# Key-query products of two chunks on four quarters of TensorE, in two PSUM banks, and a new search of the order

## The chip, the cores and the metric

The kernel runs on one core of one Trainium2 chip. Its time is the device time of one execution in microseconds; the lower, the better. A core has TensorE (PE in the profile, with its weight loads as PEld), VectorE (DVE), ScalarE (ACT), GpSimd (POOL) and SyncE (SP), which here only issues DMAs. Each engine works through its own list of instructions in the order in which they were written, and waits on semaphores where an operand is not there yet.

## The reference

Two stages in one kernel: a gated linear attention (4 batches, 8 heads, 768 steps, head size 48), then a gated convolution with a matmul, and a normalised two-layer network with a residual (model width 384, inner width 1536).

```python
f = 1.0 / (1.0 + np.exp(-f_logit))
for t in range(S):
    state = f[:, :, t, :, None] * state + np.einsum('bhd,bhe->bhde', k[:, :, t], v[:, :, t])
    y[:, :, t] = np.einsum('bhd,bhde->bhe', q[:, :, t], state)
...
x = np.ascontiguousarray(attn_out.transpose(0, 2, 1, 3)).reshape(B, S, H * D)
gate = 1.0 / (1.0 + np.exp(-gate_pre))      # gate_pre: causal convolution of x, 5 taps
x = gate * (x @ w_val) @ w_out
xn = (x - mu) / np.sqrt(var + 1e-06) * g_ln
return x + np.maximum(xn @ w_ch1, 0.0) @ w_ch2
```

## The kernel before

The 3072 tokens are cut into 24 attention tiles of 128 tokens and 12 groups of 256 tokens; a group is two tiles. A tile has two chunks of 64 tokens (`c`), four pairs of heads (`n`), and the two heads of a pair (`hh`), one on partitions 0 to 47 and one on 64 to 111.

Attention per tile. `prep` brings gates, keys and queries into the form with features on the partitions (on PE for the first eight tiles, on DVE after that) and makes `ft`, `kt`, `mv`, `gs`, `fc` on DVE, with two scans per tile. `at_t` turns `kt` on PE; ACT copies the result to `kn`. `at_a` makes the key-query products: for each chunk, pair and head one fp32 matmul with 64 columns of `kt` as weights and 64 columns of `mv` moving, 16 in all, all into one PSUM bank; ACT copies each half of the bank (64 partitions by 512) over `mv`, and POOL masks it (`affine_select`). `at_d` makes the increments of the state (16 matmuls of 48 columns) and runs the recurrence over chunks on DVE and POOL. `at_y` multiplies both by the values and the state (16 matmuls, two heads side by side in the columns, over 112 or 128 rows). An fp32 matmul is two MATMUL records in the trace, so each of these blocks is 32 of them.

Network per group. `gates` is the convolution, on DVE (12 operations of 128 x 256). `val` and `x1` are the two matmuls of the gated stage, `xnt` turns the normalised rows and ACT and DVE split them in `nh` and `nl`. `c1` and `c2` are the two layers, each product as three fp32r matmuls of full width (high by high, high by low, low by high): 18 of 256 columns and 12 of 384 for each of six slices of the inner width. Between them ACT makes `hidden_hi` and DVE `hidden_lo` out of the same bank. The weights arrive as 64-bit floats and are converted on ACT, DVE and POOL (`stage`, `wt`, `w_hi`, `w_lo`) while the first groups run.

What sets the order. The program is recorded as units (`Plan`), and a planner with a price for each unit (`price`), a delay for each dependence (`wait`) and eight PSUM banks lists the units of all engines by a greedy simulation (`forward`), eight passes back and forth, then once more with the ranks of some stretches moved by the table `MOVED`. The order so found is what each engine executes; the banks that units get come out of it too. Transposes, products, sums: everything passes through one helper, so all of it has line 466 in the profile, and rows are told apart by their tiles.

In the words below, a *block* is the 32 MATMUL records of one `at_a` (key-query), `at_d` (state) or `at_y` (output); the other matmuls use the full width of PE. A *visit* is a stretch of one or more blocks with full-width matmuls on both sides.

Of the kernel before, what the change touches and what calls it, by code (L numbers as in the profile page):

```python
# [22 lines left out]
NP = H // 2  # L23
# [29 lines left out]
WARM = 1.03  # L53
SWITCH = 0.12
# [53 lines left out]
class Unit:  # L108


    def __init__(self, engine):
        self.costs = dict.fromkeys(engine.split("|"), 0.0)
        self.engine = next(iter(self.costs))
        self.calls = []
        self.delay = self.margin = 0.0
        self.deps = set()
        self.opens = None
        self.uses = set()
        self.port = False
# [13 lines left out]
class Plan:  # L133
# [43 lines left out]
    def record(self, engine, method, args, kw):  # L177
# [25 lines left out]
        for x, writes in [(x, False) for x in ins] + ([(out, True)] if on_chip(out) else []):  # L203
            r = self.region(x)
            if isinstance(r.name, int) and r.name not in u.uses:
                if not self.users[r.name]:
                    u.opens = r.name
                else:
                    u.deps.add(self.users[r.name][0])
                u.uses.add(r.name)  # L210
                self.users[r.name].append(me)
# [15 lines left out]
        if engine == "tensor" and not u.costs["tensor"] and ins[0].dtype != F32R:  # L227
            u.costs["tensor"] = SWITCH
# [16 lines left out]
    def price(self, engine, method, out, ins, n, args, kw):  # L245
        if engine == "tensor":
            if method == "transpose":
                return 0.105 * self.slow
            if ins[0].dtype == F32R:
                return (0.436e-3 * n + 0.006) * self.slow  # L250
            return (0.056 if n > D else 0.043) * self.slow
# [35 lines left out]
    def transfer(self, issued, u, out, in_):  # L287
# [9 lines left out]
        u.costs = {"wire": n / run * (11.0 + (0.0595 if run < 1024 else 0.053 if run < 2048 else 0.0705) * run) / 16e3}  # L297
# [40 lines left out]
    def forward(self, deps, users, rank):  # L338
# [13 lines left out]
        ends = [0.0] * len(held)  # L352

        def start(i, e):
# [4 lines left out]
            if u.opens is not None:  # L359
                first = sorted(banks.values())  # L360
                spare = 1 if e == "vector" else 0
                t = max(t, first[spare]) if len(first) > spare else NEVER
# [19 lines left out]
        while len(order) < len(units):  # L382
            best = None
            for e in ENGINES:
                for i in waiting[e]:
                    t = (start(i, e), ready[i] if e == "wire" else rank[i])
                    if (best is None or t < best[0]) and fits(i, e):
                        best = (t, i, e)
# [8 lines left out]
            end[i] = free[e] = t + u.costs[e]  # L397
# [4 lines left out]
            if u.opens is not None:  # L402
                homes[u.opens] = min(banks, key=banks.get)
                del banks[homes[u.opens]]
# [64 lines left out]
class Kernel:  # L469
# [313 lines left out]
    def at_a(self, a):  # L783
        nc = self.nc
        kt, mv = self.kt[a % 2], self.mv[a % 2]
        pa = self.bank().rearrange("p (c n t) -> p c n t", c=NC, n=NP)
        with self.unit():
            for c in range(NC):
                for n in range(NP):
                    for hh in range(2):  # L790
                        r = slice(64 * (1 - hh), 64 * (1 - hh) + D)
                        nc.tensor.matmul(
                            pa[64 * hh : 64 * hh + 64, c, n, :],
# [5 lines left out]
        for hh in range(2):  # L799
            r = slice(64 * hh, 64 * hh + 64)  # L800
            nc.scalar.copy(mv[r, hh], pa[r])
# [429 lines left out]
```

## Time and profile before

| | |
|---|---|
| time, median of 3 runs | 538.26 us (537.22 to 538.6) |
| time of the profiled execution | 538.87 us |
| its span, first to last instruction | 537.2 us |
| mean granted clock of TensorE | 0.99 |
| PE busy | 501.3 us (93%) |
| PEld busy | 477.9 us (89%) |
| DVE busy | 369.1 us (69%) |
| ACT busy | 270.6 us (50%) |
| POOL busy | 169.5 us (32%) |
| share of PE in the chain that ended last | 71% |

The span has two stretches: one until the first layer of the network starts (about 81 us), in which inputs and weights arrive and several engines wait for each other, and the rest. A matmul's duration in a row is longer than its place in the stream, because matmuls are pipelined: the distance from one start to the next is what each costs.

### The profile page before, as it was taken

The page shows a single profiled execution, that of the slowest core. Times are in us where ns is not written, and L with a number is a line of the kernel's source. Part 1 is how long each engine was busy: PE and PEld are TensorE (multiplying, and loading weights), DVE is VectorE, ACT ScalarE, POOL GpSimd, SP SyncE. Part 2 cuts the span into 40 slices and gives each one's busy share as a digit, 9 for nine tenths or more (in the row PEclk, how much of TensorE's full clock was granted, in tenths as well). Part 3 has the DMA queues.
Part 4 walks back from the last instruction along what each step waited for, and adds up shares of the span by engine and source line. Part 5 has one row for each costly group of instructions (what it writes and reads, how often), then busy time and mean ns, then how long its engine had stood idle before and what let it go on. Part 6 is the DMA issues. An engine that isn't in the chain of part 4 may idle for free.

```text
span 537.2 us, 13413 instructions
## 1 busy us (share of the span) xinstructions
PE 501.3 (93%) x5272; PEld 477.9 (89%) x5272; DVE 369.1 (69%) x737; ACT 270.6 (50%) x591; POOL 169.5 (32%) x312
## 2 busy tenths in 40 slices
PE   2987689999999999999999999999999999999994
PEld 1776579999999999999989999999989999999993
DVE  5898989999884975874889733985793542543411
ACT  2598879995472453453486222543552542512210
POOL 3365676245340422230277001231421431300000
PEclk9998989999999999999999999999999999999998
DMA  6985786973454234133143610162110100000001
GB/s 137 177 172 106 190 214 173 234 227 83 103 145 94 51 85 92 39 100 70 38 114 73 149 47 1 31 156 60 24 39 9 23 31 2 9 31 1 29 1 35
DMA packets 94560, 45.60 MB, mean 85 GB/s; under 512 B 56341, under 2 KB 94485, under 8 KB 94490
## 3 DMA queue, kind: packets, MB, share of 16 engines
q1 hardware_dynamic: 94490, 44.67, 34.8%
q8 instruction: 43, 0.70, 0.6%
q14 instruction: 27, 0.22, 0.2%
HBM read 38.75 MB, written 4.72 MB: 81 GB/s over the span
## 4 chain that ended last, share of the span: by engine, by line
PE 71%; DVE 12%; DMA 4%; POOL 4%; ACT 3%; issue 2%; SPq 2%; DVEq 0%; POOLq 0%; ACTq 0%
PE ps L466 71%; DVE ps L466 4%; SPq L466 2%; POOL rs L466 2%; DVE mv L466 2%; DMA raw_q<-in_q 1%; DVE wt L466 1%; DMA xt<-x 1%; DMA stage<-in_moe_w_ch 1%; DVE gs L466 1%; ACT xn L466 1%; DVE bns L466 1%; DMA raw_f<-in_f_logit 1%; DMA out_x<-x 1%; DVE nl L466 1%
## 5 line engine op out<-in xcount | busy, mean ns | idle before, releaser
L466 PE MATMUL ps<-nh,w_hi 128*128 128x256 f32 x432 | 123.5, 286 | 0.4 <-DVE nl L466 0.3
L466 PE MATMUL ps<-nl,w_hi 128*128 128x256 f32 x432 | 121.1, 280 | 0.4 <-DVE nl L466 0.3
L466 PE MATMUL ps<-nh,w_lo 128*128 128x256 f32 x432 | 120.9, 280 | 0.0
L466 PE MATMUL ps<-w_hi,hidden_hi 128*128 128x384 f32 x288 | 99.3, 345 | 0.0
L466 DVE SCALAR_TENSOR_TENSOR hidden_lo<-ps,hidden_hi 128x512 fp32r<-128x512 f32 x72 | 49.2, 684 | 70.3 <-ACT hidden_hi L466 70.2
L466 PE MATMUL ps<-w_hi,hidden_lo 128*128 128x384 f32 x288 | 96.9, 337 | 0.0
L466 PE MATMUL ps<-w_lo,hidden_hi 128*128 128x384 f32 x288 | 96.8, 336 | 0.0
L466 ACT ACTIVATE hidden_hi<-ps 128x512 fp32r<-128x512 f32 x72 | 42.9, 595 | 85.7 <-PE ps L466 84.4
L466 PEld LDWEIGHTS ps<-nh,w_hi 128*128 128x128 f32 x432 | 81.3, 188 | 1.8 <-DVE nl L466 0.5
L466 PEld LDWEIGHTS ps<-nh,w_lo 128*128 128x128 f32 x432 | 82.1, 190 | 0.0
L466 PEld LDWEIGHTS ps<-nl,w_hi 128*128 128x128 f32 x432 | 81.2, 188 | 0.9 <-DVE nl L466 0.9
L466 DVE SCALAR_TENSOR_TENSOR ps<-xt,convw,ps 128x256 f32<-128x256 f32 x144 | 65.7, 483 | 3.5 <-ACT ps L466 1.8
L466 POOL TENSOR_SCALAR_AFFINE_SELECT mv<-mv 64x512 f32<-64x512 f32 x48 | 32.2, 671 | 86.6 <-ACT mv L466 84.9
L466 PEld LDWEIGHTS ps<-w_hi,hidden_hi 128*128 128x128 f32 x288 | 54.1, 188 | 1.1
L466 PEld LDWEIGHTS ps<-w_lo,hidden_hi 128*128 128x128 f32 x288 | 54.2, 188 | 0.0
L466 PEld LDWEIGHTS ps<-w_hi,hidden_lo 128*128 128x128 f32 x288 | 54.1, 188 | 0.0
L466 POOL TENSOR_TENSOR sd<-sn,fc 112x192 f32<-112x192 f32 x43 | 22.7, 529 | 69.8 <-DVE sn L466 54.9
L466 ACT COPY kn<-ps 64x192 f32<-64x192 f32 x96 | 30.1, 313 | 14.1 <-PE ps L466 12.9
L466 DVE TENSOR_TENSOR_SCAN gs<-ps,ends 128x511 f32<-128x511 f32 x24 | 29.1, 1214 | 9.3 <-ACT ps L466 8.9
L466 DVE TENSOR_TENSOR mv<-ps,ft 64x512 f32<-64x512 f32 x48 | 33.0, 688 | 2.5 <-PE ps L466 1.0
L466 PE MATMUL ps<-xh,wv_hi 128*128 128x256 f32 x108 | 32.7, 302 | 0.9 <-DVE gt L466 0.9
L466 PE MATMUL ps<-xl,wv_hi 128*128 128x256 f32 x108 | 31.4, 291 | 0.0
(102 smaller groups left out, 993.8 us busy)
## 6 DMA issues: line engine op xcount, KB each, us to landing
stage<-in_moe_w_ch SPq DMA_DIRECT2D x24, 384.0 KB, 4.5
st<-in_v SPq DMA_DIRECT2D x96, 48.0 KB, 2.5
out_x<-x SPq DMA_DIRECT2D x24, 192.0 KB, 1.9
raw_f<-in_f_logit SPq DMA_DIRECT2D x32, 96.0 KB, 2.3
raw_k<-in_k SPq DMA_DIRECT2D x32, 96.0 KB, 2.3
raw_q<-in_q SPq DMA_DIRECT2D x32, 96.0 KB, 2.4
raw_f<-in_f_logit SPq DMA_DIRECT2D x32, 80.0 KB, 2.2
raw_k<-in_k SPq DMA_DIRECT2D x32, 80.0 KB, 2.4
```

The source lines that it names most:

```text
L466: getattr(getattr(self.nc, engine), method)(*args, **kw)
```

## The change

Three things.

First, `at_a` opens two banks, one for each chunk, and gives the second chunk the other two of PE's four 64 x 64 quarters: output partitions are `64 * (c ^ hh)` and up, where they were `64 * hh` and up for both chunks. The loop runs over pairs outside and chunks inside, so that four matmuls that follow each other go to four quarters. ACT empties each of the four pieces by a copy of 64 x 256, where it made two copies of 64 x 512.

Second, the planner's model: it charges a change of PE's tiling (`TILING`, at the moment of the change, by mode: full width, quarters, halves) where it charged each such unit 0.12; it prefers units in the mode that PE is in (`STAY`); a unit can open more than one bank; a matmul with at most 48 rows is priced 0.03, not 0.056 or 0.043; transposes 0.102, not 0.105; full-width matmuls a little less (`WARM`); DMA a little slower.

Third, the table `MOVED` was searched anew under that model, which changes the order on every engine.

```diff
-WARM = 1.03
-SWITCH = 0.12
+WARM = 1.01
+TILING = (0.117, 0.092, 0.092)
+STAY = 3.0
...
 MOVED = (
-    (416, 8, -12), (2566, 20, -8), (22, 6, 5), (1533, 20, -20), (1524, 40, 8), (1231, 3, 8),
+    (1, 6, -5), (25, 12, 8), (156, 1, 8), (183, 12, 20), (316, 2, -5), (342, 6, 12), (387, 4, 2),
...
-        if engine == "tensor" and not u.costs["tensor"] and ins[0].dtype != F32R:
-            u.costs["tensor"] = SWITCH
+        if engine == "tensor" and method == "matmul" and ins[0].dtype != F32R:
+            u.mode = 1 if ins[0].ap[0][1] <= 64 else 2
...
-                return 0.105 * self.slow
+                return 0.102 * self.slow
...
-            return (0.056 if n > D else 0.043) * self.slow
+            return (0.03 if len(ins) and ins[0].ap[0][1] <= D else 0.056 if n > D else 0.043) * self.slow
...
+        def cost(i, e):
+            u = units[i]
+            return u.costs[e] + (TILING[u.mode] if e == "tensor" and u.mode != mode else 0.0)
+
+        def urgency(i, e):
+            if e == "wire":
+                return ready[i]
+            return rank[i] + (STAY if e == "tensor" and units[i].mode != mode else 0.0)
...
-        pa = self.bank().rearrange("p (c n t) -> p c n t", c=NC, n=NP)
+        pa = [self.bank()[:, 0 : NP * C].rearrange("p (n t) -> p n t", n=NP) for c in range(NC)]
+        half = lambda c, hh: slice(64 * (c ^ hh), 64 * (c ^ hh) + 64)
         with self.unit():
-            for c in range(NC):
-                for n in range(NP):
+            for n in range(NP):
+                for c in range(NC):
                     for hh in range(2):
                         r = slice(64 * (1 - hh), 64 * (1 - hh) + D)
                         nc.tensor.matmul(
-                            pa[64 * hh : 64 * hh + 64, c, n, :],
+                            pa[c][half(c, hh), n, :],
                             kt[r, n, c * C : c * C + C],
                             mv[r, hh, c, n, :],
                             start=True,
...
-            nc.scalar.copy(mv[r, hh], pa[r])
+            for c in range(NC):
+                nc.scalar.copy(mv[r, hh, c], pa[c][half(c, hh)])
```

How the order moves, at three places. Names: `mv`, `kt`, `st`, `kn` are the operands of the blocks, `xh`, `wv` those of `val`, `xn` the normalised rows, `ps_` a PSUM bank. On PE, around the key-query block of the ninth tile, before:

```order
L466 MATMUL ps_161<-w_5_hi,hidden_lo 128x384
L466 MATMUL ps_158<-ident,xn_145 128x128 x3
L466 MATMUL ps_159<-ident,kt_116 128x112 x4
L466 MATMUL ps_161<-mv_114,kt_116 64x64 x16
L466 MATMUL ps_158<-xh,wv_hi 128x256
L466 MATMUL ps_158<-xl,wv_hi 128x256
```

and on PE around the block of the same tile now (the two rows of banks 160 and 157 repeat four times):

```order
L483 MATMUL ps_157<-ident,xn_145 128x128 x3
L483 MATMUL ps_158<-mv_115,st_113 48x64 x16
L483 MATMUL ps_161<-ident,xn_146 128x128 x3
L483 MATMUL ps_160<-mv_114,kt_116 64x64 x2
L483 MATMUL ps_157<-mv_114,kt_116 64x64 x2
...
L483 MATMUL ps_158<-st_112,kn_121 48x48 x16
L483 MATMUL ps_163<-ident,kt_117 128x112 x4
L483 MATMUL ps_161<-nh_147,w_0_hi 128x256
```

The key-query block stood alone between full-width matmuls; now it alternates between two banks, and the state block of the same tile follows it directly, in one visit. Counted from the first `c1` matmul on, 52 blocks made 50 visits before and make 36 now: of the 16 joins now, 11 are between key-query or state blocks, or between two output blocks, and 5 between an output block and one of the others; before there was one of each. In both orders 7 key-query blocks stand ahead of the first `c1` matmul and 17 behind it.

On DVE, ahead of the second `nl` (the last operand that the first `c1` matmul waits for), before:

```order
L466 SCALAR_TENSOR_TENSOR gs<-ps_160,ends 128x511
L466 TENSOR_TENSOR nl_149<-ps_163,nh_147 128x3x128
L466 TENSOR_TENSOR kt_117<-ps_161,gs 128x512
L466 TENSOR_TENSOR gt<-gt,ps_157 128x256
L466 TENSOR_TENSOR nl_149<-ps_164,nh_147 128x3x128
```

and on DVE at the same place now:

```order
L483 SCALAR_TENSOR_TENSOR gs<-ps_163,ends 128x511
L483 TENSOR_TENSOR gt<-gt,ps_161 128x512
L483 TENSOR_TENSOR nl_149<-ps_160,nh_147 128x3x128
L483 SCALAR_TENSOR_TENSOR wt<-ps_162,wt 128x384
L483 TENSOR_TENSOR kt_117<-ps_158,gs 128x512
L483 TENSOR_SCALAR lows<-gs 128x8
L483 CAST w_0_hi<-wt 128x2x192
L483 RECIPROCAL starts<-lows 128x8
L483 TENSOR_TENSOR gt<-gt,ps_161 128x256
L483 SCALAR_TENSOR_TENSOR wt<-ps_162,wt 128x384
L483 SCALAR_TENSOR_TENSOR ft<-ps_163,starts 128x512
L483 TENSOR_TENSOR nl_149<-ps_162,nh_147 128x3x128
```

The scan to `ft` and the parts before it have moved ahead of the second `nl`. Not counting the memsets at the start, 128 instructions stood ahead of that `nl` on DVE and 133 do now: in come a scan to `ft` with its `lows` and `starts`, a subtraction to `xl`, one of 128 x 512 to `gl`, one to `wv_lo`, a combination to `wt` and two shifts to `wt`; out go a rounding to `w_hi`, two subtractions to `w_lo` and an addition to `sn`. Ahead of the eighth `hidden_lo` it was 215 and is 227; on ACT, ahead of the eighth `hidden_hi`, 211 and 232, with one more load of its function table.

On ACT, at the first key-query block, before:

```order
L466 ACTIVATE ps_162<-ps_162 128x512
L466 COPY st_112<-sd_126 48x192
L466 COPY mv_114<-ps_158 64x512 x2
L466 COPY kn_122<-ps_157 64x192 x3
L466 ACTIVATE ps_159<-ps_159 128x512
```

and on ACT at the same place now:

```order
L483 ACTIVATE ps_163<-ps_163 128x512
L483 COPY mv_114<-ps_159 64x256
L483 COPY mv_114<-ps_158 64x256
L483 COPY st_112<-sd_126 48x192
L483 COPY mv_114<-ps_159 64x256
L483 COPY kn_122<-ps_161 64x192 x4
L483 COPY mv_114<-ps_158 64x256
```

Two copies have become four, and other copies stand between them.

## Rows read from the trace of the kernel before

**Rows 1.** Busy time of each engine in three stretches: bounds, length, then engines.

```profile
0.00:81.00 81.00, 56.96 (x849) 48.85 (x849) 68.57 (x141) 57.44 (x132) 43.80 (x89) 0.96 0.77 165
81.00:125.00 44.00, 43.40 (x363) 42.61 (x358) 42.83 (x93) 42.06 (x91) 20.11 (x27) 1.00 0.74 201
125.00:529.20 404.20, 400.62 (x4067) 386.38 (x4065) 256.47 (x502) 171.12 (x371) 105.57 (x197) 1.00 0.23 57
```

**Rows 2.** Timeline around the start of the first layer: start, duration, engine, what.

```profile
80.30 0.56 DVE L466 TENSOR_TENSOR nl<-ps,nh 128x384 fp32r<-128x384 f32 x1 [0.36 <-ACT nh L466]
...
81.05 0.38 PE L466 MATMUL ps<-nh,w_hi 128*128 128x256 f32 x1
```

**Rows 3.** Timeline of PE around a key-query block that stands alone.

```profile
247.37 0.34 PE L466 MATMUL ps<-w_lo,hidden_hi 128*128 128x384 f32 x1
247.54 0.34 PE L466 MATMUL ps<-w_hi,hidden_lo 128*128 128x384 f32 x1
247.81 1.15 PE L466 MATMUL ps<-mv,kt 48*64 48x64 f32 x32
...
249.17 0.34 PE L466 MATMUL ps<-w_lo,hidden_hi 128*128 128x384 f32 x1
```

**Rows 4.** Timeline of PE from 247.75 to 247.85: what has started by then.

```profile
247.81 0.27 PE L466 MATMUL ps<-mv,kt 48*64 48x64 f32 x2
```

**Rows 5.** Timeline of PE: four transposes of 112 columns.

```profile
251.08 0.55 PE L466 MATMUL ps<-ident,kt 112*128 112x112 f32 x4
```

**Rows 6.** Timeline of PE from 24.1 to 25.0: an early block, waiting for its second head.

```profile
24.22 0.32 PE L466 MATMUL ps<-mv,kt 48*64 48x64 f32 x2
```

**Rows 7.** Timeline of PE: an output block, whose two heads share their rows.

```profile
241.31 1.10 PE L466 MATMUL ps<-mv,st 112*48 112x64 f32 x32
```

**Rows 8.** Timeline of PE around a state block that stands alone.

```profile
253.44 0.28 PE L466 MATMUL ps<-nh,w_lo 128*128 128x256 f32 x1
253.65 0.92 PE L466 MATMUL ps<-st,kn 64*48 64x48 f32 x32
...
254.72 0.29 PE L466 MATMUL ps<-nl,w_hi 128*128 128x256 f32 x1
```

**Rows 9.** Timeline of PE around a state and a key-query block in one visit.

```profile
393.81 0.28 PE L466 MATMUL ps<-nh,w_lo 128*128 128x256 f32 x1
394.02 0.92 PE L466 MATMUL ps<-st,kn 64*48 64x48 f32 x32
394.77 1.11 PE L466 MATMUL ps<-mv,kt 48*64 48x64 f32 x32
...
396.04 0.29 PE L466 MATMUL ps<-nl,w_hi 128*128 128x256 f32 x1
```

**Rows 10.** Groups by line and shape, DVE: busy, mean ns | idle before.

```profile
L466 DVE TENSOR_TENSOR_SCAN ft<-ps,starts 128x512 f32<-128x512 f32 x24 | 29.1, 1214 | 0.4
...
L466 DVE TENSOR_TENSOR sn<-sd,ps 112x192 f32<-112x192 f32 x44 | 15.2, 345 | 15.0 <-POOL sd L466 7.3 <-PE ps L466 6.4 <-ACT gh L466 1.1
...
L466 DVE TENSOR_SCALAR wt<-stage 128x384 uint16<-128x384 uint16 x13 | 6.4, 492 | 0.1
...
L466 DVE RECIPROCAL starts<-lows 128x8 f32<-128x8 f32 x24 | 4.5, 186 | 0.2
L466 DVE TENSOR_TENSOR w_lo<-wt,w_hi 128x384 fp32r<-128x384 f32 x8 | 4.4, 546 | 0.0
...
L466 DVE TENSOR_TENSOR gl<-gt,gh 128x512 fp32r<-128x512 f32 x6 | 4.1, 688 | 2.1 <-ACT gh L466 2.1
...
L466 DVE TENSOR_TENSOR xl<-xt,xh 128x768 fp32r<-128x768 f32 x2 | 1.9, 944 | 0.1
```

**Rows 11.** Groups by line and shape, ACT: two copies out of PSUM, and the table.

```profile
L466 ACT COPY kn<-ps 64x192 f32<-64x192 f32 x96 | 30.1, 313 | 14.1 <-PE ps L466 12.9
L466 ACT COPY mv<-ps 64x512 f32<-64x512 f32 x48 | 27.8, 579 | 5.1 <-PE ps L466 4.2
...
L466 ACT ACT_TABLE_LOAD x1 | 1.3, 1283 | 1.6 <-DVE ps L1017 1.6
```

More of the change, by code (lines that the diff above doesn't have):

```diff
@@ L116, in __init__ @@
         self.deps = set()
-        self.opens = None
+        self.opens = []
+        self.mode = 0
         self.uses = set()
@@ L206, in record @@
                 if not self.users[r.name]:
-                    u.opens = r.name
+                    u.opens.append(r.name)
                 else:
@@ L296, in transfer @@
         issued.margin = 0.0 if local else MARGIN
-        u.costs = {"wire": n / run * (11.0 + (0.0595 if run < 1024 else 0.053 if run < 2048 else 0.0705) * run) / 16e3}
+        u.costs = {"wire": n / run * (11.0 + (0.0595 if run < 1024 else 0.053 if run < 2048 else 0.0705) * run) / 14.5e3}
         u.delay = 1.2
@@ L352, in forward @@
         ends = [0.0] * len(held)
+        mode = 0
+        def cost(i, e):
[5 more added lines that the diff above has]
+            return rank[i] + (STAY if e == "tensor" and units[i].mode != mode else 0.0)
         def start(i, e):
@@ L358, in start @@
                 t = max(t, port[other[e]])
-            if u.opens is not None:
+            if u.opens:
                 first = sorted(banks.values())
-                spare = 1 if e == "vector" else 0
+                spare = len(u.opens) - (0 if e == "vector" else 1)
                 t = max(t, first[spare]) if len(first) > spare else NEVER
@@ L385, in forward @@
                 for i in waiting[e]:
-                    t = (start(i, e), ready[i] if e == "wire" else rank[i])
+                    t = (start(i, e), urgency(i, e))
                     if (best is None or t < best[0]) and fits(i, e):
@@ L396, in forward @@
             order.append(i)
-            end[i] = free[e] = t + u.costs[e]
+            end[i] = free[e] = t + cost(i, e)
+            if e == "tensor":
+                mode = u.mode
             if e == "sync":
@@ L401, in forward @@
                 port[e] = end[i] + 0.05
-            if u.opens is not None:
-                homes[u.opens] = min(banks, key=banks.get)
-                del banks[homes[u.opens]]
+            for r in u.opens:
+                homes[r] = min(banks, key=banks.get)
+                del banks[homes[r]]
             for r in u.uses:
```

17 rows, old and new, of the table MOVED are left out of this document.

## Prediction
> **What bounds the kernel now.** I first read busy time by stretches [rows 1]. Behind 125 us PE is busy 400.62 of 404.20 us, between 81 and 125 us 43.40 of 44.00: from 81.05 us on, where the first layer starts [rows 2], whatever is taken off PE's stream comes off the time, less new waits; only 4.2 us are idle there (44.00 - 43.40 and 404.20 - 400.62). The granted clock column is 1.00 in both, the full level of 2.4 GHz. Ahead of 81 us PE is busy 56.96 of 81.00 us and is not the bound: DVE is busy 68.57 us, and the first `c1` matmul at 81.05 follows an `nl` of DVE that starts at 80.30 and lasts 0.56 [rows 2]. Between 81 and 125 us DVE (42.83 of 44.00) and ACT (42.06) are as full as PE. So there are two regimes: a front set by what DVE has queued ahead of the first layer, and a long rest set by PE.
>
> I then read single blocks on PE, because the change works on them: 32 MATMUL records from the first to the last start, and what lies around them.
>
> **The change part by part.**
>
> *Key-query blocks.* The block at 247.81 lasts 1.15 us [rows 3]; a record in it lasts 0.22 or more (0.27 in the opening [rows 4]), so its starts span 0.93 us. One after another they would take longer: transposes of 112 fp32 columns start every 0.10 us ((0.55 - 0.26)/3, taking 0.26 for the last record [rows 5]), 0.86 ns a column, so 32 records of 64 columns would take 1.77 us. Two quarters are thus at work at once, and a pair of records costs 0.058 us (0.93/16). Will four quarters work at once? Two things have to hold. First, quarters that share rows must not hinder each other. In the output block both heads use the same rows, side by side in the columns, and its 32 records of 64 columns start within 0.88 us (1.10 - 0.22, [rows 7]): also two at a time. In the key-query block the two quarters use different rows, also two at a time. The new block is both together. Second, PE must start a later matmul ahead of an earlier one whose quarter is busy: a call is two records on one quarter. In an early block, where the second head's operand is late, the first call alone takes 0.32 us for two records [rows 6]; where nothing is late, two have started and ended within 0.27 us [rows 4], so the second is that of the other quarter. PE overtakes one call; for four quarters it must overtake three, which the trace doesn't show. Bounds: 16 pairs become 8 fours at the same 0.058, saving 0.47, less two more starts in a row, so 0.45 us a block; or nothing, if the fours don't form. A loss has a reason against it: the starts are no more than before, and the quarters at least as many. I take 0.45, because both kinds of neighbour run at the same 0.055 to 0.058. 17 blocks lie behind the first `c1`: 17 x 0.45 = **7.7 us**. The seven ahead of it lie beside DVE's work and count nothing; if that cover were gone they would add 3.2.
>
> The Trainium skill speaks against this ("TensorE: Matmul & The Clock Gate", Part 3, "What overlaps and what doesn't"): weight loads overlap matmuls in flight only when the row group differs, and two of the four quarters always share theirs. By that rule the fours would fall into pairs and the 7.7 would be nothing; the output block, whose pair shares all its row groups [rows 7], disagrees with it as far as pairs go.
>
> *Fewer visits.* A block costs PE more than its records, by what surrounds it. Key-query alone, from the last full-width start ahead of it to the second behind it: 249.17 - 247.54 = 1.63; state alone 254.72 - 253.44 = 1.28; both in one visit 396.04 - 393.81 = 2.23 [rows 3, 8, 9]. One visit fewer also has two places of full-width matmuls fewer in this count, 2 x 0.17 (247.54 - 247.37, [rows 3]). Joining saves 1.63 + 1.28 - 2.23 - 0.34 = 0.34 us, taken as 0.33. This holds for joins of the same kind of tiling. For an output block joined to another kind I take half, 0.17, between nothing and 0.33. The order has 11 joins of the first kind and 5 of the second behind the first `c1`, against 1 and 1 before: 10 x 0.33 + 4 x 0.17 = **4.0 us** (3.3 to 4.6).
>
> *Two copies become four.* A copy of 64 x 512 takes 0.579, one of 64 x 192 takes 0.313 [rows 11]; in between, 64 x 256 gives 0.313 + 64 x 0.83 ns = 0.37. A block costs ACT 4 x 0.37 - 2 x 0.58 = 0.31 us more, 7.4 in all 24. Behind 125 us ACT is busy 171 of 404 us and hides it; POOL's masks start 0.16 later and the output blocks stand several us behind. Without that cover it would cost 17 x 0.31 = 5.3. The second bank can make PE wait: nothing in the idle 4.2 us names a bank, and a wait would be at most the four copies, 1.5 us a time. I take nothing, and up to two such waits for the range.
>
> *The order in front.* This is the part that goes against the change. 133 instructions stand on DVE ahead of the second `nl`, 128 before. In come a scan (1.21), `xl` (0.94), `gl` (0.69), a remainder like `w_lo` and a combination of the same size (0.55 each), two shifts (0.49 each), and `lows` and `starts` (0.19 each at most): 5.3 us. Out go two `w_lo` (0.55 each), a rounding that I set equal to them, and `sn` (0.35): 2.0. The difference is 3.3, less some 0.06 by which instructions on DVE overlap, five times: **3.0 us** later [rows 10]. Nothing covers it: DVE sat idle for 12.4 us of the first 81 (81.00 - 68.57), most of it at the very start, before the inputs. At least nothing is lost if all of it fits in that idle time. At most it is 5.9: ahead of the eighth `hidden_lo` 12 more instructions stand on DVE, at the 0.49 us of the mean one in front (68.57/141); by then PE has more of its own work in front of it too, so I don't take that. One more table load on ACT, 1.28 us [rows 11], falls before the first inputs are there or just behind; nothing for it, 1.3 at most, inside the same range.
>
> *The sum*, against the profiled execution of 538.87: 538.87 - 7.7 - 4.0 + 3.0 = 530.2. The median of the runs, 538.26, is 0.6 lower, so I predict **529.5 us**.
>
> **The rivals.**
>
> *A: the fours don't form.* The chip keeps two quarters busy, by the trace's lack of any case with four. 538.26 - 4.0 + 3.0 = 537.3. For it: overtaking three calls is unproved. Against it: pairs of both kinds run freely. Chance 0.11.
>
> *B: starts are the limit.* The closest mean spacing in the trace is that of the state block, (0.92 - 0.21)/31 = 0.023 us [rows 8]; if 32 starts need 0.71, a block saves 0.22 and not 0.45, 3.7 in place of 7.7: 533.5. Against it, two records start together in [rows 4]. Chance 0.09. The same page of the Trainium skill (Part 1) states a floor of about 25 ns from start to start; the state block's 23 is already below it.
>
> *C: the front costs nothing.* DVE's added work fits its idle time, or PE's saved work in front counts after all: 538.26 - 11.7 = 526.6, and down to 525 with a part of the seven front blocks. For it, 12.4 us of idle on DVE; against it, most of them precede the first input. Chance 0.15.
>
> *D: slower, the full engines between 81 and 125 us.* DVE and ACT are both at 96 to 97% there. Ahead of the eighth layer output DVE has 12 more instructions and ACT 21 (mostly the halved copies). If PE's wait in that stretch is the sum of both, and not the larger: 12 x 0.65, at the mix of scans and copies named above, and 21 x 0.37, is 7.8 + 7.8 = 15.6, and the 3.0 is in it: 538.26 - 11.7 + 15.6 = 542.2. It decides from 11.7 us of new waits on. Against it: the two engines work side by side on the same slices, so their delays mostly coincide. Chance 0.07.
>
> **How the numbers follow.** Forecast 0.58, A 0.11, B 0.09, C 0.15, D 0.07. The forecast's own range, with the front at 0 to 5.9, joins at 3.3 to 4.6 and two waits for a bank, is 526 to 536. A and C lie at its edges; leaving out D and the farther half of A and C, the 80% range is **524.5 to 536.8**. About 0.3% (1.6 us) is what a measurement of this kernel tells from no change. Faster by more than that (below 536.6): forecast, B, C, and a fifth of A, **0.84**. Within it: most of A, **0.09**. Slower: D, **0.07**.
>
> **What would show it.** In the profile after: the starts of a key-query block spanning about 0.48 us where they span 0.93 (step one; 0.71 is B, 0.93 is A); a joined visit of state and key-query about 1.5 us long; the first `c1` matmul at about 84 us (81 is C, 87 or more speaks for D); PE's idle time behind that matmul still near 4 us; ACT's busy time up by some 7 us; the copies of 64 x 256 at 0.37. The prediction is wrong if fours don't form, or if PE's idle time behind the first layer grows by 5 us or more, which the rows of before can't show since the order there is new.

## The result and the profile after

The changed kernel takes 530.83 us (530.59 to 532.16, 4 runs) where the kernel before, run beside it, takes 537.74 (536.99 to 538.6): a ratio of 0.988, with a 95% interval of 0.985 to 0.990. The forecast was 529.5 us, with a range of 524.5 to 536.8. The profiled execution took 530.6 us, with a span of 528.9.

Busy time by stretches, columns as in [rows 1]. The stretches are cut at the first `c1` and at the last start of `c2`. First the kernel before, cut that way, then the kernel after:

```profile
0.00:81.05 81.05, 57.01 (x850) 48.85 (x850) 68.62 (x141) 57.49 (x132) 43.85 (x89) 0.96 0.77 165
81.05:125.00 43.95, 43.35 (x361) 42.60 (x358) 42.78 (x93) 42.01 (x91) 20.06 (x27) 1.00 0.74 202
125.00:528.80 403.80, 400.28 (x4066) 386.36 (x4065) 256.45 (x501) 171.12 (x371) 105.57 (x197) 1.00 0.23 57
```

```profile
0.00:84.99 84.99, 58.78 (x850) 49.79 (x850) 69.18 (x143) 58.84 (x142) 42.34 (x91) 0.88 0.69 147
84.99:125.00 40.01, 37.83 (x343) 35.88 (x340) 37.76 (x80) 37.45 (x82) 25.08 (x34) 1.00 0.87 226
125.00:520.90 395.90, 394.65 (x4085) 383.91 (x4084) 264.22 (x514) 184.10 (x418) 94.90 (x186) 1.00 0.25 60
```

The two regimes of the forecast are both there. The front got longer, from 81.05 to 84.99 us (+3.94). Behind it PE is busy 432.48 us (37.83 + 394.65) instead of 443.63 (43.35 + 400.28), 11.15 less, and its idle time went from 4.12 to 3.43 us. So the late stretch is 11.84 us shorter, and 11.84 - 3.94 = 7.9 us is left. The spans differ by 8.3 us (537.2 and 528.9); the other 0.4 lies behind the last `c2`. The medians of the runs differ by 6.9 us only, mostly because the profiled execution of the kernel before took 1.1 us more than its median (538.87 and 537.74).

What the late stretch gained can be split by the groups on PE behind the first `c1` (line, engine, operands, shape, count | busy, mean ns | idle before). Before:

```profile
L466 PE MATMUL ps<-mv,kt 48*64 48x64 f32 x544 | 19.5, 221 | 0.0
L466 PE MATMUL ps<-st,kn 64*48 64x48 f32 x548 | 15.9, 207 | 0.0
```

After:

```profile
L483 PE MATMUL ps<-st,kn 64*48 64x48 f32 x548 | 15.6, 206 | 0.4 <-ACT gt L483 0.4
L483 PE MATMUL ps<-mv,kt 48*64 48x64 f32 x544 | 12.6, 224 | 0.6 <-DVE hidden_lo L483 0.5
```

The 544 key-query records (17 blocks of 32) do as much work as before, each for as long (221 and 224 ns), but together they hold PE for 12.6 us instead of 19.5: 6.9 us less, by being side by side. The other 4.25 us of the 11.15 lie outside this group; what part of them the visits make is asked in e4. One key-query block that stands alone, in the timeline of PE (start, duration, what), and what had started 25 ns after its first start:

```profile
234.65 0.28 PE L483 MATMUL ps<-nh,w_lo 128*128 128x256 f32 x1
234.86 0.69 PE L483 MATMUL ps<-mv,kt 48*64 48x64 f32 x32
235.49 0.38 PE L483 MATMUL ps<-nh,w_hi 128*128 128x256 f32 x1
```

```profile
234.86 0.29 PE L483 MATMUL ps<-mv,kt 48*64 48x64 f32 x4
```

It lasts 0.69 us where [rows 3] had 1.15. The 32 starts span 0.477 us (0.69 less the last record's own time), and four records, not two as in [rows 4], have started in the first 25 ns. The single starts show the rhythm behind the first four: three steps of 6 to 7 ns, then one of 38 to 39, so a four every 58 ns where before it was a pair every 58 ns. Two of the 17 blocks pause in the middle; they start at 87.80 and 307.13 us and last 1.09 and 1.02 us.

On ACT the copies are what was forecast, 0.367 us each:

```profile
L483 ACT COPY mv<-ps 64x256 f32<-64x256 f32 x96 | 35.2, 367 | 11.3 <-PE ps L483 9.3
```

### The profile page after: what moved, and what is told of

It is laid out like the page before. It is cut to its first block, busy times and chain, and to the rows that moved or that the text cites. A ratio compares the mean times of both kernels' runs of the same rounds, so it can differ in the third digit from the quotient of the medians.

```text
span 528.9 us, 13475 instructions
## 1 busy us (share of the span) xinstructions
PE 491.8 (93%) x5272; PEld 469.7 (89%) x5272; DVE 372.4 (70%) x739; ACT 280.4 (53%) x640; POOL 162.3 (31%) x310
## 4 chain that ended last, share of the span: by engine, by line
PE 77%; DVE 9%; POOL 4%; ACT 4%; DMA 2%; issue 2%; SPq 0%; DVEq 0%; POOLq 0%; ACTq 0%
PE ps L483 77%; DVE ps L483 2%; DVE mv L483 1%; POOL rs L483 1%; DVE wt L483 1%; ACT xn L483 1%; DVE gs L483 1%; DVE ft L483 1%; ACT ps L483 1%; DMA stage<-in_moe_w_out 1%; DMA raw_q<-in_q 1%; POOL mv L483 0%; DMA stage<-in_moe_conv_w 0%; DVE kt L483 0%; DMA xt<-x 0%
## 5 line engine op out<-in xcount | busy, mean ns | idle before, releaser
L483 DVE SCALAR_TENSOR_TENSOR ps<-xt,convw,ps 128x256 f32<-128x256 f32 x144 | 64.2, 485 | 6.6 <-ACT ps L483 4.7
L483 POOL TENSOR_TENSOR sd<-sn,fc 112x192 f32<-112x192 f32 x42 | 21.3, 508 | 65.6 <-DVE sn L483 44.8
L483 ACT COPY mv<-ps 64x256 f32<-64x256 f32 x96 | 35.2, 367 | 11.3 <-PE ps L483 9.3
L483 POOL TENSOR_SCALAR rs<-bna 128x1 f32<-128x1 f32 x24 | 4.6, 191 | 102.3 <-DVE bna L483 101.7
```

Of the source, the lines that this page charges most:

```text
L483: getattr(getattr(self.nc, engine), method)(*args, **kw)
```

## The experiments

### Are the quarters the cause, or the new order? (e1)

The order, the two banks and the four copies stay; both chunks go to the same two quarters.

```diff
-        half = lambda c, hh: slice(64 * (c ^ hh), 64 * (c ^ hh) + 64)
+        half = lambda c, hh: slice(64 * hh, 64 * hh + 64)
```

> The kernel after with one thing undone: both chunks of a tile go to the same two quarters of PE (the two halves hh alone choose the quarter), in the order, the two banks and the four copies of the kernel after. The output is the reference's. Theory (the quarters make the time): a key-query block spans 0.93 us from its first start to its last again instead of 0.477; 17 blocks stand behind the first c1, so the late stretch gets 17 x 0.45 = 7.7 us longer and the time is about 538.3 us (537.3 to 539.5), that is the time of before, although the new order is kept. Rival (the new order and the two banks make it, not the quarters): the block hardly matters and the time stays at 530.8 (530.3 to 531.5).

Measured: 538.68 us, ratio to before 1.002 (1.0005 to 1.0035); set against the ratio of after, 0.988, that is 1.4%, or 7.7 us, more. The spans of the profiled executions are 6.0 us apart (528.9 and 534.9), but that of e1, at 536.61 us, was one of its faster ones. The same group on PE behind the first `c1` of e1, and the stretch from there on:

```profile
L483 PE MATMUL ps<-mv,kt 48*64 48x64 f32 x544 | 19.7, 221 | 0.5 <-DVE hidden_lo L483 0.4
```

```profile
85.18:527.00 441.82, 439.42 (x4426) 427.29 (x4422) 301.87 (x593) 219.82 (x499) 120.26 (x220) 1.00 0.29 74
```

19.7 us against 12.6, and PE is busy 439.42 us instead of 432.48, 6.94 more. The quarters make this part of the gain, and without them the new order is worth nothing as a whole: against the kernel before, PE is busy 4.2 us less behind the first `c1`, and that matmul comes 4.1 us later (85.18).

### How far ahead does PE look for a free quarter? (e2)

```diff
-            for n in range(NP):
-                for c in range(NC):
+            for c in range(NC):
+                for n in range(NP):
```

> The kernel after with the loops inside the key-query block turned: all four head pairs of the first chunk, then all four of the second, so neighbouring records use two quarters for 16 records and then the other two. Same units, same order of units, same quarters, banks and copies; the output is the reference's. Theory (PE starts a matmul beside its predecessors only if it is among the next few): a block spans about 0.9 us again, the time is 537.3 to 538.5 us. Rival (PE looks far ahead and fills the idle quarters from behind): a block stays at 0.48 us and the time at 530.8. In between, an overlap at the seam of the chunks alone would give 0.85 us and 536.5 to 537.

Measured: 534.33 us, ratio 0.9954 (0.9939 to 0.9969), between the two theories. The group behind the first `c1` of e2:

```profile
L483 PE MATMUL ps<-mv,kt 48*64 48x64 f32 x544 | 16.8, 224 | 0.9 <-DVE hidden_lo L483 0.9
```

And the timeline of PE cut off 0.31 us after a block's first start, in e2 and then in e1:

```profile
236.25 0.57 PE L483 MATMUL ps<-mv,kt 48*64 48x64 f32 x12
```

```profile
236.03 0.51 PE L483 MATMUL ps<-mv,kt 48*64 48x64 f32 x10
```

In e2 the first 16 records of the program use two quarters, at a pair every 58 ns, so ten of them have started 0.31 us into the block, as in e1. Twelve have started: the two extra ones must be the first pair of the second chunk, which stand behind all 16, since the first chunk's two quarters are taken (the rows don't name the quarter). PE let them pass the six that had not started yet. By the end of the first chunk six records of the second had started beside it, so three of the sixteen steps of 58 ns disappear: the starts span 0.757 us instead of 0.93. My "in between" of 0.85 allowed an overlap at the seam alone and was too small. So PE does look ahead, by some six records here, which is more than the fours need, and not far enough to find a free quarter 16 records on.

### What is a visit worth? (e4)

Between two joined blocks the next full-width matmuls are issued, if nothing forbids it.

```diff
-        self.nc.issue(order, engines)
+        self.nc.issue(self.nc.apart(order, homes), engines)
+    def apart(self, order, homes):
...
+                if u.mode and seen:
...
+                        del order[q]
+                        order.insert(p, x)
```

> The kernel after, with the joins taken out: where two blocks of small tiles follow each other on PE, the next matmuls of full width (c1, c2, v, x or transposes) are issued between them, where nothing forbids it; behind the first c1 PE then visits the small tiling 50 times instead of 36, as before did. The work, the quarters, the banks and the engines are the kernel's own; the output is the reference's. Theory (each way into and out of a tiling costs): 14 visits by 0.17 to 0.33 us are 2.4 to 4.6 us, the time 533.2 to 535.4, most likely 534.8. Rival (the joins are worth nothing, other moves of the order made the gain in the gaps): 530.8 (to 531.5). Units issued earlier than planned may wait for their inputs; such waits show in the list of waits and are taken off.

Measured: 539.12 us, ratio 1.004 (1.0026 to 1.0055), more than expected. The stretches behind the first `c1`, which stands at 86.83:

```profile
86.83:125.00 38.17, 36.01 (x332) 34.09 (x329) 35.93 (x78) 35.62 (x79) 24.03 (x33) 1.00 0.88 224
125.00:530.00 405.00, 401.27 (x4095) 386.18 (x4094) 266.51 (x516) 185.94 (x422) 96.27 (x187) 1.00 0.23 60
```

PE is busy 437.28 us there, 4.80 more than in the kernel after, for the same matmuls and 14 more visits: 0.34 us a visit. It is idle for 5.89 us instead of 3.43, and the first `c1` is 1.84 us later, probably because units were pulled ahead of their inputs, which was not followed up. Those two come from the way the joins were undone; the 4.80 us are the price of the visits. The rival (joins worth nothing) is out.

### Do the four copies cost anything? (e3)

The kernel before, in its own order, with its copies halved.

```diff
+            if method == "copy" and engine == "scalar" and tuple(args[0].shape) == (64, NC, NP, C):
+                for c in range(NC):
+                    self.nc.scalar.copy(args[0][:, c], args[1][:, c])
+                continue
```

> The kernel before in its own order and on its own quarters, but each 64x512 copy of the key-query product on ACT is made as two of 64x256: the part of the change that costs something, alone. The output is the reference's. Theory (ACT's slack hides it): 24 x 2 more copies, ACT busy up by 24 x 0.31 = 7.4 us (270.6 to about 278), the stretch behind the first c1 unchanged within 0.5 us, the first c1 later by 0 to 2 us because ACT is fuller there; the time 537.7 to 539.5. Rival (ACT stands on the path where attention is dense): 17 x 0.31 = 5.3 us late and 7 x 0.31 = 2.2 in front, the time up to 545.

Measured: 537.24 us, ratio 1.0002 (0.999 to 1.0013). Nothing, as forecast. The copies in e3:

```profile
L466 ACT COPY mv<-ps 64x256 f32<-64x256 f32 x96 | 30.5, 366 | 5.2 <-PE ps L470 4.5
```

They take 0.366 us each as well, but two that follow each other on the same 64 partitions overlap by about 0.1 us, so ACT is busy 30.5 us with them and not 35.2; the whole of ACT rose only from 270.6 to 273.5 us. The 7.4 us of my sum came about only in the new order.

### What made the front late? (e5, e6)

The start of ACT's timeline in the kernel after:

```profile
7.47 1.28 ACT L483 ACT_TABLE_LOAD   x1 [7.47 <-DMA stage<-in_moe_conv_w]
8.76 0.51 ACT L483 ACTIVATE ps<-stage 5x384 f32<-5x384 f32 x1
9.22 1.10 ACT L483 ACTIVATE wt<-stage 5x384 f16<-5x384 f32 x2
10.33 1.28 ACT L483 ACT_TABLE_LOAD   x1
11.63 0.58 ACT L483 ACTIVATE ps<-ps 128x512 f32<-128x512 f32 x1
```

The new order puts the convolution weights ahead of the first tile's Sigmoid. So ACT first loads a table for the conversions, and only then, ahead of the Sigmoid, a second one. The kernel before did it the other way round: one load of 1.28 us [rows 11], at 1.56 us, and the Sigmoid at 9.48. In e5 a Sigmoid of one column stands ahead of everything:

```diff
+        self.tc.nc.vector.memset(self.rs[0], 0.0)
+        self.tc.nc.scalar.activation(self.rs[1], self.rs[0], AF.Sigmoid)
```

> The kernel after with two instructions put ahead of everything: DVE clears a 128x1 tile and ACT takes its Sigmoid, so that ACT loads the table of the Sigmoid while it has nothing else to do. In the trace of after ACT's first work is the conversion of the convolution weights, with a table load of 1.28 us at 7.47 us, and a second load of 1.28 us at 10.33 us ahead of the first tile's Sigmoid, which starts at 11.63 us; in before there is one load, at 1.56 us, and that Sigmoid starts at 9.48 us. Theory (these loads are the larger part of the late front): the Sigmoid starts at 9.5 to 10.1 us, DVE's first scan 1.5 to 2.2 us earlier, the first c1 at 82.8 to 83.5 us instead of 84.99, the late stretch is unchanged, the time 528.6 to 529.4. Rival (the front is set by DVE's count of instructions and by loads that come later, and takes the 2 us up again): the first c1 at 84.5 to 85.5, the time 530.8.

Measured: 528.73 us, ratio 0.985 (0.9834 to 0.9866). ACT's timeline in e5:

```profile
0.81 1.28 ACT L1036 ACT_TABLE_LOAD   x1 [0.81 <-PEq L1237]
2.10 0.20 ACT L1036 ACTIVATE rs<-rs 128x1 f32<-128x1 f32 x1
7.61 0.50 ACT L483 ACTIVATE ps<-stage 5x384 f32<-5x384 f32 x1 [5.30 <-DMA stage<-in_moe_conv_w]
8.05 1.09 ACT L483 ACTIVATE wt<-stage 5x384 f16<-5x384 f32 x2
10.10 0.58 ACT L483 ACTIVATE ps<-ps 128x512 f32<-128x512 f32 x1 [0.96 <-PE ps L483]
```

One load is left, and the Sigmoid starts at 10.10 instead of 11.63 us. It now waits 0.96 us for PE, so what is left to the 9.48 of the kernel before is not ACT's doing. (The Trainium skill, "ScalarE: Activation LUTs", "Table sets: the hidden batching unit", says that cheap functions such as the copy are in every set; the trace agrees, since behind the Sigmoid's table no other is loaded.) The first `c1` came at 82.56. E6 was to test the cause that the prediction had named, the number of instructions on DVE:

```diff
+        left = {"wv_lo": 1, "xl": 2}
+        for i in order:
...
+            if method == "tensor_sub" and left.get(name, 0):
+                left[name] -= 1
+                engines[i] = "gpsimd"
```

> The kernel after with three subtractions of the front put on POOL instead of DVE, as before had them: one wv_lo (128x432 elements) and the first two groups' xl (128x768, 0.9 us each on DVE); nothing else moves. The output is the reference's. Theory of the prediction (DVE's count of instructions ahead of the second nl sets the first c1): DVE has 1.5 to 2.2 us less ahead of it and the first c1 comes up to that much earlier, at 83 to 84 us, the time 529 to 530. Rival (DVE's idle time at the very start is what came on top, not the count): the first c1 within 0.5 us of 84.99, the time 530.5 to 531.2. POOL takes about 1.9 us for an xl, which can delay the products that read it: then 531 to 533.

Measured: 533.18 us, ratio 0.9932 (0.9912 to 0.9951), and the first `c1` at 85.56, no earlier. But e6 didn't make DVE's work less. Up to the end of the second `nl` DVE is busy 70.69 us, where it is 69.79 in the kernel after. With the subtractions gone, a `BATCH_NORM_STATS2` that starts at 75.39 us in the kernel after started at 74.32, 1.07 earlier. Then this followed, in e6 (POOL, DVE) and in the kernel after (DVE):

```profile
74.75 1.81 POOL L483 TENSOR_TENSOR xl<-xt,xh 128x768 fp32r<-128x768 f32 x1
74.80 2.00 DVE L483 TENSOR_SCALAR wt<-stage 128x384 uint16<-128x384 uint16 x1
```

```profile
74.52 0.94 DVE L483 TENSOR_TENSOR xl<-xt,xh 128x768 fp32r<-128x768 f32 x1
75.86 0.37 DVE L483 TENSOR_SCALAR wt<-stage 128x384 uint16<-128x384 uint16 x1
```

Beside POOL's `xl` DVE's shift took 2.00 us instead of 0.37, and the lead was gone: the next instruction starts at 76.70, where it is 76.12 in the kernel after. The kernel before, with an `xl` of the front on POOL, shows the same once:

```profile
66.95 1.84 POOL L466 TENSOR_TENSOR xl<-xt,xh 128x768 fp32r<-128x768 f32 x1
67.40 1.65 DVE L466 TENSOR_SCALAR wt<-stage 128x384 uint16<-128x384 uint16 x1
```

No other of these shifts takes more than 0.54 us in the three kernels. PE also waits 1.6 us in front for `xl` (0.6 in the kernel after) and behind the first `c1` 1.4 us for an `xn` of POOL. So e6 is no test of DVE's count: it shows that an `xl` on POOL costs a shift of DVE beside it more than DVE saves. What DVE's count alone is worth stays open.

One profile of each is little to go by in the front, so the kernels after (f1) and e5 (f2) were run again on one chip.

> The kernel after, unchanged, on one chip with f2 and f3, so that the three can be set against each other without a change of chip. Expected: 530.8 us, ratio to before 0.988.

> The kernel of e5, unchanged. Theory (the two table loads in a row cost the front what the first c1 moved): 2.0 to 2.4 us below f1. Rival (e5's gain was mostly the chip's): less than 1 us below f1.

Measured: f1 530.32 us, ratio 0.9883 (0.9862 to 0.9903); f2 529.68, ratio 0.9852 (0.9835 to 0.9869). F1 came out as expected. The medians of f1 and f2 are only 0.64 us apart, which is what the rival said (less than 1 us); by the ratios it is 1.7 us (0.9883 - 0.9852, of 537), and their intervals overlap. The stretch up to the first `c1` in the profiled executions, the first of before's order, the others of after's:

| kernel | table loads behind 7 us | first tile's Sigmoid, us | first `c1`, us | granted clock up to it | DVE busy up to it, us |
|---|---|---|---|---|---|
| before | 0 | 9.48 | 81.05 | 0.96 | 68.62 |
| after | 2 | 11.63 | 84.99 | 0.88 | 69.18 |
| f1 (after again) | 2 | 11.70 | 84.57 | 0.94 | 69.17 |
| e5 | 0 | 10.10 | 82.56 | 0.94 | 69.23 |
| f2 (e5 again) | 0 | 10.17 | 84.34 | 0.86 | 69.34 |

At the start the two loads cost 1.53 us each time (11.63 - 10.10 and 11.70 - 10.17). What of that arrives at the first `c1` differs: e5, at a mean clock of 0.94, is 2.01 us ahead of f1, while f2, at 0.86, is 1.78 us behind e5, of the same kernel. These are the two rows:

```profile
0.00:82.56 82.56, 55.73 (x849) 47.07 (x849) 69.23 (x144) 57.77 (x142) 43.17 (x91) 0.94 0.70 152
```

```profile
0.00:84.34 84.34, 59.80 (x850) 51.06 (x850) 69.34 (x144) 57.85 (x142) 42.32 (x91) 0.86 0.68 148
```

PE does the same matmuls and is busy 4.07 us longer, because more of them ran at 1.2 GHz. Most of f2's delay arises between 45 and 66 us, first e5, then f2:

```profile
45.00:66.00 21.00, 15.53 (x243) 13.38 (x243) 18.80 (x40) 17.62 (x42) 11.64 (x19) 0.84 0.66 159
```

```profile
45.00:66.00 21.00, 17.22 (x199) 15.23 (x192) 16.97 (x36) 16.26 (x38) 9.76 (x16) 0.59 0.61 150
```

The granted clock is 0.59 instead of 0.84 there, and DVE gets 1.83 us less done. Between 30 and 40 us, where DVE in f2 is still 0.25 us ahead of e5, f2's clock is already the lower one (0.66 and 0.83). So the slower clock fits as the cause. It isn't all: the kernel after has its first `c1` only 0.42 us behind f1, at 0.88 and 0.94, and e1 and e2, with two loads, a clock of 0.94 and blocks that last longer, have theirs at 85.18 and 85.73. So the early table load is a gain at the start; in the end it is 2.10 us between the medians of e5 and after, which did not run side by side (1.4 by the ratios, whose intervals overlap), and 0.64 us between f2 and f1 on one chip. Its size can't be given more closely here, and the 2.0 to 2.4 expected of f2 was missed. Which pause lets the clock fall in one run and not in another stays open.

### The same change for the state block (e7, e8, e9, f3)

If the mechanism is what it seems, the state block should gain by it as well. E7 gives it two banks and swaps the halves of the second chunk; DVE then adds that chunk in two parts (and POOL clears the two small `sn` tiles once at the start).

```diff
-        psd = self.bank()[:, 0 : NC * NP * D].rearrange("p (c n e) -> p c n e", c=NC, n=NP)
+        psd = [self.bank()[:, 0 : NP * D].rearrange("p (n e) -> p n e", n=NP) for c in range(NC)]
...
-            for c in range(NC):
-                for n in range(NP):
+            for n in range(NP):
+                for c in range(NC):
...
-                        o = 64 * (1 - hh)
+                        o = 64 * (c ^ 1 ^ hh)
...
-                nc.vector.tensor_add(new[0:112], sd[0:112], psd[0:112, c])
+                if c == 0:
+                    nc.vector.tensor_add(new[0:112], sd[0:112], psd[c][0:112])
+                else:
+                    with self.unit():
+                        for o in (0, 64):
+                            nc.vector.tensor_add(new[o : o + D], sd[o : o + D], psd[c][64 - o : 64 - o + D])
```

> The kernel after with the state block (at_d) treated as the change treats the key-query block: two banks, the second chunk's outputs on the swapped halves, the four quarters in turn; the second chunk's addition on DVE becomes two of 48x192, which read the bank at the other partitions. The planner orders it with the same table of moves, which was not made for it. The output is the reference's. Theory (any block of the small tiling whose records have 64 rows or fewer gains when four quarters are in use): the state block spans 0.36 us instead of 0.70, 17 blocks behind the first c1 are 5.8 us; the order visits the small tiling 43 times instead of 36 there, 1.2 to 2.3 us; DVE has 24 x 0.25 = 6 us more work, some 2 us of it in the front. Sum 530.8 - 5.8 + 1.8 + 1 to 2 = 528 to 529 us. Rival (the order is worth more than the block): the order falls apart and the time is 531 to 535 although the block gets shorter.

Measured: 557.88 us, ratio 1.0378 (1.0341 to 1.0415), far slower. The state group behind the first `c1`, and the stretches:

```profile
L483 PE MATMUL ps<-st,kn 64*48 64x48 f32 x544 | 9.9, 209 | 0.9 <-ACT kn L483 0.8
```

```profile
0.00:95.83 95.83, 63.42 (x850) 54.20 (x850) 75.54 (x157) 63.75 (x151) 40.39 (x89) 0.77 0.67 151
95.83:125.00 29.17, 27.20 (x229) 26.14 (x230) 24.88 (x49) 25.91 (x58) 13.13 (x20) 0.94 0.63 175
125.00:549.90 424.90, 408.77 (x4194) 392.42 (x4194) 285.19 (x562) 192.12 (x436) 102.31 (x194) 1.00 0.23 60
```

The block did what it should: 9.9 us instead of 15.6; alone it starts a four every 45 ns. But the table of moves was made for another kernel. The first `c1` comes at 95.83, and behind it PE is idle for 18.1 us (454.07 - 435.97). E8 tells the planner the block's new duration (the line shown, against the kernel after), loads the table first as e5 does, and has an order of its own: a new table of moves, searched by random changes and the planner's own costs; e9 has another table from the same search.

```diff
-            return (0.03 if len(ins) and ins[0].ap[0][1] <= D else 0.056 if n > D else 0.043) * self.slow
+            return (0.03 if len(ins) and ins[0].ap[0][1] <= D else 0.056 if n > D else 0.024) * self.slow
```

> The state block in fours as in the run e7, the table of the Sigmoid loaded first as in e5, the planner told the state block's new duration (0.024 us a call instead of 0.043), and an order searched anew for this kernel (36 visits of the small tiling behind the first c1, as in the kernel after). The output is the reference's. Theory (e7 fell to its order, not to the block): the 17 state blocks behind the first c1 take 0.37 instead of 0.70 us each, 5.6 us less than e5; the second addition on DVE and an order searched for less long cost 0 to 3 us; the time is 523.1 to 526.1 us. Rival (the state block's two banks are what cost e7 its time, whatever the order, because PE or DVE wait for a free bank): PE idles 5 us or more behind the first c1 again and the time is 528.7 or above.

> The same kernel as e8 with another table of moves from the same search, which the planner holds for 0.6 us slower; 37 visits behind the first c1. The output is the reference's. If the block decides and orders of about equal rank are alike, the time is within 1.5 us of that of e8; if single waits decide, it differs by more, in either direction.

> The kernel of e8, unchanged. In the profile the state blocks gave 6.0 us behind the first c1 and the front took 3.8 us of them back. Expected: 1 to 2.2 us below f2, at 526.5 to 527.8.

Measured: e8 527.49 us, ratio 0.9823 (0.9802 to 0.9844); e9 527.35, ratio 0.983 (0.9803 to 0.9857); f3, which is e8 beside f1 and f2, 527.07, ratio 0.981 (0.9795 to 0.9825), whose interval lies below those of f1 and f2. This is the fastest kernel here, 3.25 us below f1. It is 2.6 us below f2, more than the 1 to 2.2 expected, at a time inside the range given; e8 missed the 523.1 to 526.1 expected of it. E9 is 0.14 us from e8, within the 1.5 expected of orders of about equal rank. F3's state group and stretches:

```profile
L827 PE MATMUL ps<-st,kn 64*48 64x48 f32 x544 | 9.6, 208 | 0.0
```

```profile
0.00:86.50 86.50, 58.79 (x849) 49.13 (x850) 76.12 (x157) 58.19 (x144) 42.02 (x91) 0.86 0.68 151
86.50:125.00 38.50, 37.72 (x345) 35.92 (x346) 37.26 (x85) 36.45 (x81) 20.54 (x29) 1.00 0.83 227
125.00:517.30 392.30, 389.99 (x4079) 378.19 (x4077) 276.44 (x535) 184.35 (x416) 89.03 (x179) 1.00 0.23 59
```

The state blocks give 6.0 us (15.6 to 9.6). PE's idle time behind the first `c1` is 3.1 us, so the two banks are no hindrance in an order made for them; the rival is out, and e7 fell to its order. Of what is missing, a good part went into the front: DVE is busy 76.12 us ahead of the first `c1` instead of 69.34 (f2), and that matmul comes at 86.50 instead of 84.34.

## Why the prediction was right, point by point

*Two regimes.* Right for the late one. Everything taken off PE behind the first `c1` came off the time: 11.15 us less busy time there, 11.84 us less in all, and idle time fell from 4.12 to 3.43 instead of growing. For the front, see below.

*Key-query blocks, 7.7 us.* The block alone is what was forecast, starts spanning 0.477 us against 0.48. Over 17 blocks the group gave 6.9 us; most of the missing 0.8 is in the two blocks that pause (1.09 and 1.02 us instead of 0.69). Undone alone (e1) it cost 7.7 us in the runs' ratios, 7.1 in the group and 6.94 in PE's busy time. The doubtful step, whether PE may pass three calls with busy quarters, holds with room to spare (e2: six records). The rule of the Trainium skill that was set against it ("TensorE: Matmul & The Clock Gate", Part 3, "What overlaps and what doesn't") would have made it nothing; four starts within 20 ns, two by two on the same rows, disagree. The same section of the Trainium skill has matmuls start strictly in the order of the program; e2's block, where two pass six, disagrees as well.

*Fewer visits, 4.0 us.* Right in size: 4.25 us of PE's lower busy time are not in the key-query group, and e4, which put 14 visits back, cost PE 4.80 us, 0.34 a visit. So the half price for output blocks was probably too cautious; the full 0.33 for all 14 would have given 4.6. A joined visit of state and key-query lasts 1.40 us, against the 1.5 forecast.

*The copies, nothing.* Right: 0.367 us each, hidden in the new order (PE's waits behind the first `c1` don't name them) and free in the old one (e3). ACT's busy time rose by 9.8 us (270.6 to 280.4), where some 7 were forecast; 7.4 are the copies and 1.3 the table load.

*The front, +3.0 us.* The size was near (+3.94 in the profile), the reason mostly not, so that the size came near is luck. The step counts DVE's work up to the second `nl`. Up to the end of it, before and after:

```profile
0.00:80.86 80.86, 56.82 (x846) 48.72 (x847) 68.43 (x141) 57.30 (x131) 43.66 (x89) 0.96 0.77 165
```

```profile
0.00:85.60 85.60, 59.16 (x850) 49.97 (x850) 69.79 (x145) 59.45 (x143) 42.87 (x92) 0.88 0.69 147
```

That end came 4.74 us later, of which DVE's busy time is 1.36 (68.43 to 69.79) and not 3.0. The shifts to `wt` were mis-sized: two more of them were put at 0.49 each, a mean that holds the one of 1.65 us beside POOL's `xl`. Now no shift runs beside such an `xl`, and the six take 2.29 us in all, where the four of before took 2.74. DVE's idle time, which the step left as it was, rose by 3.38 us (12.43 to 15.81). Of this 1.87 lies in the first 20 us (DVE busy 13.73 before, 11.86 after; 13.21 in e5). The failed step is therefore the sentence on the table load, which put it ahead of the inputs or "just behind" and priced it at nothing, 1.3 at most: it fell on the chain, and two loads in a row stand ahead of the Sigmoid, which moved from 9.48 to 11.63, of which e5 took back 1.53. Where the other 1.5 us of idle time come from was not separated. The lower granted clock (0.88 against 0.96) is one candidate; DVE's waits for POOL's `sd` (1.7 us, 0.3 before) and for ACT's `xn` (0.8, not listed before) are others. The prediction also put most of DVE's 12.4 us of idle time at the very start; the first 10 us of the kernel before hold 5.4 of them.

The end of the front looks different as well. The first `c1` matmul does not wait for the second `nl` now; the next one does:

```profile
84.13 0.92 PE L483 MATMUL ps<-st,kn 64*48 64x48 f32 x32
84.99 0.38 PE L483 MATMUL ps<-nh,w_hi 128*128 128x256 f32 x1
85.65 0.39 PE L483 MATMUL ps<-nl,w_hi 128*128 128x256 f32 x1 [0.28 <-DVE nl L483]
```

*The rivals.* A and B are out: fours form, and starts follow each other by 6 to 7 ns. C is out in its pure form, since the front did cost something. D's mechanism didn't appear: between 85 and 125 us PE is idle 2.18 us, against 0.60 in the like stretch of before, and DVE and ACT are both 94% busy and no longer 96 to 97.

The sum was right because two terms were close and the third came near for the wrong reason.

## What to carry to other kernels

A small-tile block is worth cutting into as many independent quarters as its rows and columns allow, interleaved within some six records; count the gain only where PE is the bound. When an order is made anew, look at the first instructions of each engine too: what stands first on ACT chooses the first table, and a load that was free at 1.5 us can land on the chain. And before work is moved from DVE to POOL, look at what DVE does beside it: e6 lost there what it had gained. A changed block in an order made for another can lose far more than it gains (e7: 5.7 us gained in the block, 27 us lost in all), so a change of the work and a search of the order belong together.

## What the runs showed of the hardware

- Starts on different quarters follow each other by 6 to 7 ns, for four in a row (2 to 4 in places of e2); a four of 64 columns comes every 58 ns and one of 48 columns every 45 (e7), the same rhythm that pairs keep in the kernel before.
- PE starts a matmul ahead of six earlier ones whose quarters are busy (e2), but none of the second chunk started while eight or more of the first had not.
- 96 copies at 0.366 us kept ACT busy 30.5 us in e3, where two that follow each other read the same 64 partitions of one bank, and 96 at 0.367 took 35.2 us in the kernel after, where they read two banks. One bank is not enough: the two copies of a block in the kernel before read its two halves and don't overlap (48 at 0.579 us, 27.8 us busy).
- A shift of 128x384 on DVE (`wt<-stage`, 16-bit numbers) takes 0.34 to 0.53 us in before, after and e6; the two that ran beside an `xl` of POOL took 1.65 (before) and 2.00 (e6). Why was not tested.
- The granted clock of the front differs from execution to execution of one kernel, 0.94 in e5 and 0.86 in f2 up to the first `c1`, which came 1.78 us apart.
